# First quarter of w_in loaded ahead of two value loads, two pairs of odd-value copies moved from GpSimd to VectorE, a query copy moved up and one mask product repeated, in a fused windowed-attention and two-layer kernel

## The chip, the cores and the metric

The kernel runs on one core of one Trainium2 chip. The metric is the device time of one execution in microseconds (us); less is better. Times before the change: 294.75 us, the median of 5 runs (293.83 to 295.93).

The engines are named as in the profile: PE is TensorE, DVE is VectorE, ACT is ScalarE, POOL is GpSimd, SP is SyncE. All times of instructions below count from the start of the span of the profiled execution.

## What is computed

```python
# q, k, v: (8, 8, 576, 64) = batch, heads, sequence, head size; window 32
scores = (q @ k.T) / sqrt(64)
scores = where(abs(i - j) <= 32, scores, -1e9)
attn   = softmax(scores)
x      = (attn @ v) as (4608, 512)         # tokens x (heads * head size)
h      = x @ w_in                          # w_in (512, 2048)
g      = h * sigmoid(1.702 * h)
out    = g @ w_out                         # w_out (2048, 512), out (4608, 512) float32
```

## The kernel before

All work is one program for one core, in an order written out by hand: each engine runs its instructions in the order of the source, and waits on semaphores for what other engines or transfers produce. The 4608 tokens are 36 units of 128 tokens; two units make one tile of the two dense layers. The function `head` works off units 0 to 6 and the dense layers of the first tiles; `window(w)` then repeats for w = 4 to 19.

**Loads.** Nearly all are issued by POOL, in source order, and are cast to 16 bits on the way in. `load_heads("A")` and `load_heads("B")` bring the keys and queries of tokens 0 to 319 and 320 to 575 (a part of A comes through SP and ACT instead); `load_heads(1)` brings tokens 512 to 1023. `load_v(m)` brings the values of unit m into a tile `ve`; `load_v(4, 0)` brings only the first piece of unit 4, 64 rows, because unit 4 crosses from one batch into the next. `load_w_in(c)` brings the quarter c of w_in (512 of its 2048 columns, all of it for products d = 2c and 2c+1 of `layer1`), `load_w_out(c)` a quarter of w_out.

**Odd values.** A unit needs its values a second time, shifted by 64 tokens, in a tile `vo`. `odd_v(m, eng)` (L163) makes it with two copies of 64 x 528: the lower half of `ve` of unit m, and the upper half of `ve` of unit m+1. So `odd_v(2)` needs values 3, and `odd_v(3)` needs the first piece of values 4. Units 0 and 1 are copied by DVE and ACT, units 2 and 3 by POOL (before the change), the later ones by DVE.

**Block B, the stretch that the change touches.** After the values of units 0 and 1 the head prepares the keys and queries of block B for units 2 and 3. For each of four pairs of heads hp: `pair_heads` copies the loaded rows into an order fit for the transpose (tiles `kc`, `qc`, on DVE, 64 x 512); `rows_T` transposes them on PE into a PSUM bank (four transposes, L179) and copies the bank out to `kT` on DVE or to `qT` on ACT (L105). The banks are few: `"htho"[hp]` and `"hoth"[hp]` name them, "h" with two buffers, "t" and "o" with one. So the key transposes of hp = 2 wait for the copy `kT` of hp = 0, and the query transposes of hp = 2 (bank "t") wait for the copy `kT` of hp = 1 on DVE.

**Masks.** For units 0 to 3 the mask is not applied by a multiplication: `blind(u)` writes large negative numbers into both score banks (`sc`, eo = 0 and 1) by a product of an identity and the tile `neg`, 128 x 512, that starts the accumulation (L227), and `scores(u)` adds the products of keys and queries on top. Later units use a mask tile, made on POOL by `setup_mask` and `cut_mask`, and first read by `band(4)`.

**After block B.** `scores(2)`, `scores(3)`, then `layer1(0, 0)` (PE product with w_in, ACT for the activation, L313 and L315), `values(2)` (L273), `norm(2)` on DVE (L284, L285), `layer1(0, 1)`, `values(3)`, `norm(3)`, `x_T(2)` (transposes, L300), `layer1(0, 2)`, `x_T(3)`, `layer1(0, 3)` and from there a long run of products. `keep_busy(n)` issues n products of zeros of 128 x 512 whose results nobody reads (L418).

Of the kernel before, what the change touches and what calls it, by code (L numbers as in the profile page):

```python
# [21 lines left out]
SQ = 64  # L22
# [5 lines left out]
class _Kernel:  # L28
# [181 lines left out]
    def setup_neg(self):  # L210
# [4 lines left out]
        for b in range(2):  # L215
            for half in range(2):
# [2 lines left out]
                pool.affine_select(out=ap, in_=ap, compare_op=ALU.is_ge, fill=-30000.0, base=0,  # L219
                                   pattern=[[-sign, SQ]], channel_multiplier=sign)  # L220

    def blind(self, u):

        sc = self.sc[u] = [self.bank("a", [128, 8, SQ], F32, f"sc{eo}") for eo in range(2)]
        neg = self.neg.rearrange("k (o b) s -> k o b s", o=1).to_broadcast([128, 4, 2, SQ])
        for eo in range(2):
            self.nc.tensor.matmul(sc[eo].rearrange("k (h b) s -> k h b s", b=2), self.ident, neg,  # L227
                                  start=True, stop=False, skip_group_check=True)
# [192 lines left out]
    def head(self):  # L421

        nc, dve, act, pool = self.nc, self.nc.vector, self.nc.scalar, self.nc.gpsimd
# [8 lines left out]
            self.load_v(m)  # L432
        for c in "kq":
            self.load_heads("B", c)
        self.load_v(3)
        self.load_v(4, 0)
        for c in range(4):
            self.load_w_in(c)
        self.odd_v(2, pool)
        self.odd_v(3, pool)  # L440
        for c in (0, 2):
            self.load_w_out(c)
        self.setup_mask()
        self.cut_mask()
        for c in "kq":
            self.load_heads(1, c)
        self.load_w_out(1)
        self.load_v(4, 1)
        for m in range(5, 7):
# [30 lines left out]
        self.keep_busy(1, "h")  # L480
        for hp in range(4):
            self.pair_heads("k", "B", hp, dve)
        for hp in range(2):
            self.pair_heads("q", "B", hp, dve)
        for hp in range(4):
            self.rows_T("k", "B", hp, "htho"[hp], dve)
            if hp < 2:
                self.pair_heads("q", "B", hp + 2, dve)
            self.rows_T("q", "B", hp, "hoth"[hp], act)
        self.scores(2)  # L490
        self.scores(3)
        self.layer1(0, 0)
        self.values(2)
        self.norm(2)
# [278 lines left out]
```

## Time and profile before

| what | before |
|---|---|
| median of 5 runs, and their spread | 294.75 us (293.83 to 295.93) |
| the profiled execution: its time, its span | 295.93 us, 294.2 us |
| busy: PE, PEld, DVE, ACT, POOL | 286.7, 235.3, 187.3, 185.3, 104.1 us |
| mean granted TensorE clock | 0.994 |
| POOL, the loads of v3 and the first piece of v4 issued | 8.57 to 10.17 us |
| POOL, the four loads of w_in issued | 10.11 to 13.15 us |
| POOL, the copies for `odd_v(2)` and `odd_v(3)` | one at 13.07 us, three from 15.91 to 17.89 us |
| POOL, loads of w_out 0 and 2 issued | from 17.85 us |
| POOL, mask tile made | 19.31 to 21.52 us |

The profiled execution is the slowest of the five runs. The profile counts an engine as busy while an instruction of it is under way; PEld is PE's loading of weights. A line of the chain of waits gives start and length in us, then the engine, tile and source line that held the chain. A line of a timeline gives start, length, engine, line, operation, output and inputs, sizes and count, and in brackets the idle time before it and what ended it. In a table of stretches each engine has its busy time and, in brackets, its instructions; PEclk is the granted clock as a share of the full one.

### The profile page before, as it was taken

To read this page: it belongs to the slowest core of one execution; us is meant where nothing else is said; L and a number is where in the kernel's file an instruction comes from. 1 tells how busy PE (TensorE), PEld (TensorE's weight loads), DVE (VectorE), ACT (ScalarE), POOL (GpSimd) and SP (SyncE) were. 2 spreads that over 40 slices of the span, in tenths; PEclk is the share of its full clock that TensorE was granted. 3 is DMA by queue.
4 is the path that set the end of the run, shared out by engine and by line. 5 is a ranking of instruction groups with operands and counts; after the bars stand their busy time and mean duration, and the time that the engine had idled before them with its cause. 6 is when DMAs were issued, how large, how long until landed. Compare 5 with 4: busy or idle time off the path is not lost.

```text
span 294.2 us, 9542 instructions
## 1 busy us (share of the span) xinstructions
PE 286.7 (97%) x4020; PEld 235.3 (80%) x4020; DVE 187.3 (64%) x552; ACT 185.3 (63%) x306; POOL 104.1 (35%) x146
## 2 busy tenths in 40 slices
PE   7989999999999999999999999998999999999995
PEld 2558855775888888888888888887888888888884
DVE  3654358777485858585858585856585858583353
ACT  4666637786775757576767676766575757575330
POOL 8875435988634353433333434332000000000000
PEclk9979999999999999999999999999999999999999
DMA  9999999999999999999999999999925330303012
GB/s 147 145 207 206 200 184 129 193 141 143 151 167 164 160 148 152 174 142 203 101 165 129 170 117 142 149 139 153 161 38 145 38 109 3 108 6 107 2 71 71
DMA packets 145291, 38.83 MB, mean 132 GB/s; under 512 B 129888, under 2 KB 140896, under 8 KB 145248
## 3 DMA queue, kind: packets, MB, share of 16 engines
q0 software_dynamic: 97696, 18.16, 89.1%
q1 hardware_dynamic: 47104, 19.67, 41.3%
q8 instruction: 31, 0.51, 0.8%
q10 hardware_dynamic: 448, 0.39, 0.5%
q14 instruction: 12, 0.10, 0.2%
HBM read 36.96 MB, written 9.44 MB: 158 GB/s over the span
## 4 chain that ended last, share of the span: by engine, by line
PE 94%; DVE 2%; DMA 2%; ACT 1%; issue 1%; ACTq 0%; DVEq 0%
PE h_ps L313 43%; PE o_ps L375 32%; PE o_ps L325 7%; PE pv L273 4%; PE sc L245 4%; DMA q_raw<-in_q_dram 2%; PE tp L179 1%; PE tp L300 1%; DVE x L285 1%; ACT qT L105 1%; PE sc L227 0%; PE junk L418 0%; DVE o_sb L393 0%; DVE kT L105 0%; DVE qc L105 0%
## 5 line engine op out<-in xcount | busy, mean ns | idle before, releaser
L313 PE MATMUL h_ps<-xT,w_in_sb 128*128 128x256 bf16 x1152 | 136.3, 274 | 0.0
L315 ACT ACTIVATE g<-h_ps 128x512 f16<-128x512 f32 x144 | 85.7, 595 | 75.8 <-PE h_ps L313 74.4
L313 PEld LDWEIGHTS <-w_in_sb 128*128 128x128 bf16 x1152 | 112.6, 98 | 13.9
L160 POOL DMA_DIRECT2D ve<-in_v_dram x40 | 34.1, 858 | 83.8 <-PE pv L273 61.1
L375 PEld LDWEIGHTS <-gs 128*128 128x128 f16 x480 | 45.8, 98 | 5.8
L375 PE MATMUL o_ps<-w_sum,gs 128*128 128x256 f16 x360 | 44.3, 273 | 0.0
L251 ACT ACTIVATE p<-sc 128x512 bf16<-128x512 f32 x72 | 37.2, 604 | 2.7 <-PE sc L245 2.5
L375 PEld LDWEIGHTS <-g 128*128 128x128 f16 x360 | 34.1, 98 | 4.6 <-ACT g L315 0.2
L352 DVE TENSOR_TENSOR gs<-g 128x512 f16<-128x512 f16 x30 | 12.7, 425 | 39.1 <-ACT g L315 39.1
L285 DVE TENSOR_TENSOR x<-pv,rec 128x256 bf16<-128x256 f32 x72 | 30.6, 424 | 2.5
L375 PE MATMUL o_ps<-w_out_sb,g 128*128 128x256 f16 x240 | 29.0, 273 | 0.0
L105 DVE COPY part<-o_ps 128x256 f32<-128x256 f32 x45 | 19.1, 424 | 13.9 <-PE o_ps L375 12.6
L393 DVE TENSOR_TENSOR o_sb<-o_ps,part 128x256 f32<-128x256 f32 x45 | 19.0, 422 | 12.1 <-PE o_ps L375 11.4
L262 DVE TENSOR_TENSOR p<-p,mask 128x512 bf16<-128x512 bf16 x64 | 24.9, 427 | 1.2 <-ACT p L251 1.0
L147 POOL DMA_DIRECT2D qs<-in_q_dram x27 | 22.9, 868 | 3.2 <-DMA ks<-in_k_dram 2.8
L147 POOL DMA_DIRECT2D ks<-in_k_dram x27 | 22.8, 862 | 1.5 <-DMA ve<-in_v_dram 1.5
L325 PE MATMUL o_ps<-w_out_sb,g 128*128 128x512 f16 x96 | 23.2, 380 | 0.0
L105 DVE COPY vo<-ve 64x528 bf16<-64x528 bf16 x65 | 19.4, 298 | 2.0 <-DMA ve<-in_v_dram 0.5
L284 DVE RECIPROCAL rec<-pv 128x4 f32<-128x4 f32 x72 | 12.6, 175 | 12.0 <-PE pv L273 12.0
L412 ACT ACT_TABLE_LOAD x15 | 19.2, 1283 | 0.3
L251 ACT ACT_TABLE_LOAD x15 | 19.2, 1283 | 0.3
L273 PEld LDWEIGHTS <-p 128*64 128x64 bf16 x576 | 11.5, 111 | 7.3 <-DVE p L262 3.6
(70 smaller groups left out, 246.3 us busy)
## 6 DMA issues: line engine op xcount, KB each, us to landing
out_dram<-o_sb SPq DMA_DIRECT2D x34, 256.0 KB, 5.1
ve<-in_v_dram POOLq DMA_DIRECT2D x32, 128.0 KB, 5.8
ks<-in_k_dram POOLq DMA_DIRECT2D x22, 128.0 KB, 7.6
qs<-in_q_dram POOLq DMA_DIRECT2D x22, 128.0 KB, 9.1
w_in_sb<-in_moe_w_in_dram POOLq DMA_DIRECT2D x4, 512.0 KB, 10.8
w_out_sb<-in_moe_w_out_dram POOLq DMA_DIRECT2D x4, 512.0 KB, 12.1
ve<-in_v_dram POOLq DMA_DIRECT2D x8, 64.0 KB, 6.0
ks<-in_k_dram POOLq DMA_DIRECT2D x7, 64.0 KB, 6.7
```

What stands on the lines that cost most here:

```text
L105: (eng.copy if eng is self.nc.scalar else eng.tensor_copy)(out, in_)
L147: self.nc.gpsimd.dma_start(self.stage[key][off:off + m, n], src[b, :, s:s + m, :].rearrange("h s d -> s h d"))
L160: self.nc.gpsimd.dma_start(self.ve[m % NV][off:off + n, :, :self.D], self.v[b, :, s:s + n, :].rearrange("h s d -> s h d"))
L251: nc.scalar.activation(p[:, eo], sc[eo], AF.Exp, scale=self.scale)
L262: self.nc.vector.tensor_mul(pv, pv, msk.to_broadcast([128, 4, 2, SQ]))
L273: nc.tensor.matmul(acc[half][blk * 64:blk * 64 + 64, hh, :], p[:, h % 2, h // 2 * 2 + blk, :], vt[:, h, :D + 1], start=(hh == 0), stop=(hh ...
L285: nc.vector.tensor_mul(x[:, hs, :], acc[half][:, :, :D], rec[:, hs, :].to_broadcast([128, 4, D]))
L313: nc.tensor.matmul(hps[:, i, :], self.w_in_sb[:, kr, ff * 128:(ff + 1) * 128], self.xT[t][:, kr, :], start=(i == 0 and kr == 0), stop=(i = ...
L315: nc.scalar.activation(self.g[t][:, ffs[0]:ffs[1] + 1:ffs[1] - ffs[0], :], hps, AF.Gelu_apprx_sigmoid)
L325: nc.tensor.matmul(o_ps, self.g[t][:, ff, s * 128:(s + 1) * 128], self.w_out_sb[:, ff, :], start=(ff == 0), stop=(ff == self.NFF - 1))
L375: nc.tensor.matmul(self.part[t, key], x, y, start=(first and k == 0), stop=(k == 7), skip_group_check=True)
L412: self.nc.scalar.activation(self.spark, self.spark, AF.Gelu_apprx_sigmoid)
```

## The change

The loads: quarter 0 of w_in is issued before values 3 and the first piece of values 4 instead of after them. The two loads of keys and queries of block 1 (four transfers) are issued before the mask tile is made instead of after it. `odd_v(2)` and `odd_v(3)` are taken out of POOL's order (ahead of the loads of w_out) and given to DVE, after the scores of unit 3 and ahead of `norm(2)`. In block B the copy `qc` of hp = 2 is moved ahead of the first key copy; the copy of hp = 3 stays after it. Between the transposes of hp = 1 and hp = 2 PE repeats one product of the mask into the bank `sc` of unit 3, eo = 0, which already holds the same numbers.

```diff
+    def blind_again(self, u, eo):
+
+        neg = self.neg.rearrange("k (o b) s -> k o b s", o=1).to_broadcast([128, 4, 2, SQ])
+        self.nc.tensor.matmul(self.sc[u][eo].rearrange("k (h b) s -> k h b s", b=2), self.ident, neg,
+                              start=True, stop=False, skip_group_check=True)
...
             self.load_heads("B", c)
+        self.load_w_in(0)
         self.load_v(3)
         self.load_v(4, 0)
-        for c in range(4):
+        for c in range(1, 4):
             self.load_w_in(c)
-        self.odd_v(2, pool)
-        self.odd_v(3, pool)
         for c in (0, 2):
             self.load_w_out(c)
+        for c in "kq":
+            self.load_heads(1, c)
         self.setup_mask()
         self.cut_mask()
-        for c in "kq":
-            self.load_heads(1, c)
...
             self.pair_heads("k", "B", hp, dve)
-        for hp in range(2):
+        for hp in range(3):
             self.pair_heads("q", "B", hp, dve)
         for hp in range(4):
+            if hp == 2:
+                self.blind_again(3, 0)
             self.rows_T("k", "B", hp, "htho"[hp], dve)
-            if hp < 2:
-                self.pair_heads("q", "B", hp + 2, dve)
+            if hp == 0:
+                self.pair_heads("q", "B", 3, dve)
             self.rows_T("q", "B", hp, "hoth"[hp], act)
         self.scores(2)
         self.scores(3)
+        self.odd_v(2, dve)
+        self.odd_v(3, dve)
         self.layer1(0, 0)
```

## The prediction

> **What bounds the kernel now.** I read the page first, then the chain of waits between 14 and 25 us, then a table of stretches around it, then the timelines of DVE and POOL, and last the landing times of single transfers. The page:
>
> ```profile
> span 294.2 us, 9542 instructions
> PE 94%; DVE 2%; DMA 2%; ACT 1%; issue 1%; ACTq 0%; DVEq 0%
> ```
>
> PE holds 94% of the chain, and after 24.33 us it runs without a gap that counts. So a microsecond won in the head reaches the end, unless a transfer then comes late. The chain through block B:
>
> ```profile
> 15.36 0.23 PE tp L179 x4
> 15.59 0.02 issue
> 15.62 0.42 DVE kT L105
> 16.04 0.64 DVE qc L105
> 16.68 0.34 DVE kT L105
> 17.02 0.04 issue
> 17.06 0.29 PE tp L179 x4
> ...
> 18.17 0.58 PE sc L245 x40
> 18.75 1.82 PE h_ps L313 x8
> 20.56 0.58 PE pv L273 x8
> 21.14 1.36 PE h_ps L313 x8
> 22.50 0.38 PE pv L273 x16
> 22.88 0.33 PE tp L300 x4
> 23.21 0.87 PE h_ps L313 x8
> ```
>
> Two things are to be seen. A DVE copy of queries (0.64) stands between two key copies on the chain. And `layer1(0, 0)` takes 1.82 us for the eight products that take 0.87 at 23.21. The table of stretches says why; it is cut every 3.41 us, the length for which the half clock holds:
>
> ```profile
> 11.65:15.07 3.42, 3.26 (x32) 1.57 (x30) 2.02 (x9) 1.59 (x3) 2.14 (x4) 1.00 1.69 163
> 15.07:18.48 3.41, 2.43 (x95) 1.84 (x95) 2.79 (x8) 1.41 (x5) 2.45 (x4) 1.00 1.24 206
> 18.48:21.89 3.41, 3.41 (x54) 2.26 (x40) 0.85 (x4) 3.38 (x6) 3.06 (x12) 0.50 1.23 207
> ```
>
> After the length and the comma, the first number is PE's busy time, the third from the end the granted clock. The half clock fills 18.48 to 21.89, straight after the one stretch in which PE was busy for only 2.43 of 3.41 us. The two stretches before the first row shown, from 4.83 and from 8.24, have 3.06 and 3.08 us busy, and the clock stayed full behind them. So in this execution the limit lies between 2.43 and 3.06. How the stretches lie in other executions the trace does not show.
>
> **Part 1, the copy moved up and the POOL copies removed.** The timeline of all engines:
>
> ```profile
> 15.91 1.98 POOL L105 COPY vo<-ve 64x528 bf16<-64x528 bf16 x3 [2.13 <-DMA ve<-in_v_dram]
> 15.96 0.72 DVE L105 COPY qc<-qs 64x512 bf16<-64x512 bf16 x1
> ```
>
> This `qc` takes 0.72 us, beside a POOL copy; the two `qc` copies at 14.97 take 0.49 together, some 0.22 each from start to start. In the changed kernel the third `qc` follows them, at 15.41 to 15.69, while DVE would have waited for the first transposes anyway (ready at 15.59): up to 0.07 late. The first `kT` copy ends near 16.05 as before, one free `qc` follows (0.22 in place of 0.64), and the second `kT` copy ends near 16.64 in place of 17.02. The query transposes of hp = 2 start then: 0.38 us earlier. Everything to the end of the scores hangs on them, so scores end at 18.37, not 18.75. Between bounds: if only the order helped and not the missing POOL copy, 0.64 stays and nothing is won (0); if `kT` were not delayed at all, 0.42. I take 0.38.
>
> The Trainium skill ("SBUF — State Buffer", section "SBUF: two separate sides") says that DVE and GpSimd hold a shared pair of ports for a whole instruction, and also that a DVE copy which uses both ports keeps GpSimd from writing descriptors for its DMAs. The second half speaks against the change, which puts four such copies on DVE. The row nearest to it: POOL issued two value loads in 1.60 us at 8.57, while DVE made the copies of `odd_v(0)`, against 2.90 us for three at 4.33: no slowdown to see. By the rule POOL's issues could be about 1.2 us late there.
>
> **Part 2, the repeated product.** It is one more 128 x 512 on PE. In the chain three such products take 0.65 us, 0.22 each. PE stood idle before the key transposes of hp = 2 (0.17) and the query ones (0.69), so it lies in the gap: at most 0.1 on those key transposes, and nothing on the chain, since the query transposes wait for DVE until 16.68. If that cover were gone it would cost 0.22.
>
> **Part 3, the clock.** In the stretch 15.07 to 18.48 PE was idle for 0.98 us. The repeated product fills about 0.2, and 0.38 of the wait goes, its place taken by work that came later. The busy time comes to about 3.0, and the last 0.1 us is dense `layer1`. That is just at the lower edge of the stretches that kept the clock and far from 2.43, so I expect it to stay full. Then the chain from 18.75 to 24.33, 5.58 us, becomes three products at 0.87, two groups of values at 0.38 and two groups of transposes at 0.24: 3.85. That wins 1.73.
>
> The Trainium skill ("TensorE: Matmul & The Clock Gate", section "Why this matters for your kernels") asks only that PE has no idle gap over about 3 us. By that rule gaps of 0.17 and 0.69 us don't matter, and parts 2 and 3 would bring nothing: the sum would be 0.38. The granted clock in the table shows that they did matter. The same page (Part 4) says that transposes don't count as busy in the same way, which would fit this stretch.
>
> Does anything else hold that chain? I walked it at full clock. Scores end 18.37. `layer1(0, 0)` ends at 19.24. The exponentials (four in 2.06 us, first at 18.46 before, so 18.08) give unit 2 by 19.11 and unit 3 by 20.14. `values(2)` runs 19.24 to 19.62, `layer1(0, 1)` to 20.49, `values(3)` to 20.87, `x_T(2)` and `layer1(0, 2)` to 21.98. `norm(3)` ended 1.48 us after the start of `values(3)` before, so 21.97: in time. ACT loads its table (1.28) and runs the first activation by 22.06; `layer1(0, 3)` wants that bank at 22.22, not at 24.33. The gain at that point is 2.11 = 0.38 + 1.73.
>
> **Part 4, the loads.** The issue order decides the landing. In two narrow windows:
>
> ```profile
> w_in_sb<-in_moe_w_in_dram POOLq DMA_DIRECT2D x1, 512.0 KB, 8.0
> ve<-in_v_dram POOLq DMA_DIRECT2D x1, 64.0 KB, 6.7
> ```
>
> Quarter 0 was issued at 10.11 and landed at 18.1; the piece of v4 was issued at 9.37 and landed at 16.1; v3 (8.57, 7.2 us) at 15.8. Transfers landed in order of issue throughout the head. Exchanged, the three together still end at about 18.1: quarter 0 at about 17.5, v3 and v4 between 17.8 and 18.1. Quarter 0 is wanted at 18.37; it would have been in time even unmoved, so this brings 0 to 0.1. Quarter 1 (10.93 + 9.8 = 20.7) is wanted at 21.11.
>
> **Part 5, the copies on DVE.** Four copies at about 0.30 (six at 44.05 take 1.89). DVE was idle for 2.95 us before `norm(2)`. It finishes `kT` at 17.64; the first copy ends 17.95, the second waits for v3 and ends by 18.4 (`values(2)` wants it at 19.24), the last by 19.0. `norm(2)`, queued behind them, wants DVE at 19.53. So they cost nothing, with half a microsecond to spare. If v4 lands after 19.2, each microsecond costs one.
>
> **Part 6, POOL.** Without its 2.13 us wait POOL issues w_out earlier, but the transfers ahead of it fill the queue (205 GB/s), so landings stay. Mask building goes behind four load issues; its first reader is at 46.20. Two later transfers come near: queries of block 1 landed at 36.8 and PE wants their copy at 39.19 - 2.11 = 37.08; v7 landed at 44.8 and its copy stands ahead of `band(4)` on DVE, which would then end near 46.3, while PE reaches `values(4)` at 46.4. So about 2.2 us is all that can pass; beyond it these two hold PE.
>
> **The sum.** 295.93 - 2.11 = 293.82 us for the profiled execution, the slowest of five and 1.18 above the median. If all of that excess is the half clock, the changed kernel takes 293.82 in every run; if none, the median becomes 294.75 - 2.11 = 292.64. I take the middle, 293.2.
>
> **Rivals.** *The clock still drops.* If the limit is nearer to 3.06 than I think, or the window lies otherwise, only 0.38 is won: 294.4. For it: the margin of part 3 is thin. *The loads hold it back.* The two transfers of part 6 land half a microsecond to one later: about 294.2. *Slower:* transfers share the engines instead of landing in order, and the piece of v4 lands with quarter 1 at 20.7. Then the last copy ends at 21.0, `norm(2)` starts 1.5 us late, `x_T(2)` and the products wait, and PE's gap brings the half clock back (1.73): 293.2 + 3.2 = 296.4. It begins to count when v4 lands after 19.2, and decides from about 20.6. Against it: the strict order of landings. That the change does nothing of what it says needs `qc` to be slow without POOL too; then nothing of part 1 comes, and the clock decides alone.
>
> **How the numbers follow.** Full clock 0.66, at 292.6 to 293.8; clock still drops 0.15; later transfers take it 0.06; slower 0.13. A measurement of this kernel can tell about 0.5% (1.47 us) from no change, that is below 293.28 or above 296.22. Some 0.6 of the likeliest case lies below 293.28, and a little of the second: faster 0.42. The rest of these and the third are within: 0.45. Slower 0.13. The range 292.5 to 295.0 takes in the first three cases and leaves out the slower one and the tails.
>
> **What would show it.** Granted clock 1.00 in every stretch from 5 to 30 us; the `qc` copies at about 0.28 and no POOL copy of `vo`; `layer1(0, 0)` eight products in 0.87; `layer1(0, 3)` near 22.2; DVE's copies of `vo` waiting for v3 until about 18. I am wrong if a half clock stands anywhere in the head, if `norm(2)` starts behind a wait for `ve`, or if `kc`/`qc` of block 1 or `vo` of unit 6 hold PE near 37 or 46 us.

## The result and the profile after

| | before | after |
|---|---|---|
| median | 294.23 us (95 runs, 292.84 to 296.54) | 293.43 us (53 runs, 292.68 to 295.33) |
| ratio after to before, 95% interval | | 0.9969 [0.9959, 0.9979] |
| profiled execution: time, span | 295.93, 294.2 us | 293.43, 291.7 us |
| mean granted clock of the profiled execution | 0.994 | 0.999 |

The change wins 0.31% (0.21 to 0.41%): real, but within the 0.5% that the prediction counted as no change. The predicted 293.2 us is 0.2 us off, the range holds the time. That it is so near is partly luck. The prediction took 1.55 us off a median of 294.75 from five runs; with 95 runs the median before is 294.23, 0.52 lower, and the change took 0.80 off it. The two errors, 0.52 and 0.75, nearly cancel.

The chain of waits of the changed kernel, for the same stretch as before:

```profile
15.68 0.23 PE tp L179 x4
15.91 0.02 issue
15.93 0.42 DVE kT L105
16.36 0.19 DVE qc L105
16.55 0.34 DVE kT L105
16.89 0.04 issue
16.93 0.51 PE tp L179 x12
...
18.48 0.98 PE h_ps L319 x8
19.46 0.38 PE pv L279 x16
19.83 0.98 PE h_ps L319 x8
20.81 0.38 PE pv L279 x16
21.19 0.33 PE tp L306 x4
21.52 0.87 PE h_ps L319 x8
22.39 0.24 PE tp L306 x4
22.63 11.35 PE h_ps L319 x104
```

(Line numbers behind L221 are six higher than before, behind the head nine.) The `qc` copy between the two `kT` copies holds the chain for 0.19 us instead of 0.64. The eight products of `layer1(0, 0)` take 0.98 instead of 1.82. The long run of products starts at 22.63, before at 24.33: 1.70 us earlier, although block B itself happened to start 0.32 later (15.68 against 15.36). The table of stretches, cut at the same times as before:

```profile
15.07:18.48 3.41, 3.23 (x100) 2.16 (x100) 2.98 (x9) 1.53 (x5) 1.10 (x3) 1.00 1.66 184
18.48:21.89 3.41, 3.41 (x57) 2.72 (x58) 2.68 (x11) 3.38 (x6) 1.85 (x3) 1.00 1.24 207
```

PE is busy for 3.23 us (before 2.43), and the clock behind it is full. VectorE's timeline, with the copies taken over from POOL:

```profile
17.82 1.56 DVE L105 COPY vo<-ve 64x528 bf16<-64x528 bf16 x4
19.75 0.18 DVE L290 RECIPROCAL rec<-pv 128x4 f32<-128x4 f32 x1 [0.37 <-PE pv L279]
```

The four copies are done at 19.38, and `norm(2)`, whose first instruction is the second line, waits for PE, not for them: 0.37 us to spare, 0.5 had been worked out.

The two profiled executions lie 2.50 us apart, the medians only 0.80. Of the 2.50, 1.70 come from the head, and 1.11 from a line of the chain of before that the change has nothing to do with:

```profile
202.87 1.11 issue
```

PE stood still there in the middle of `values`, and the profile names nothing that it waited for. After has 0.31 us of such and other small pieces more than before elsewhere (1.70 + 1.11 - 2.50).

One of the runs of before that were made beside the experiments, of 298.16 us, was in a slow state and is left out of all counts and means below.

### The profile page after: what moved, and what is told of

Same layout as the page of the kernel before. It is cut to its first block, busy times and chain, and to the rows that moved or that the text cites. A ratio compares the mean times of both kernels' runs of the same rounds, so it can differ in the third digit from the quotient of the medians.

```text
span 291.7 us, 9542 instructions
## 1 busy us (share of the span) xinstructions
PE 285.6 (98%) x4021; PEld 234.5 (80%) x4021; DVE 190.1 (65%) x556; ACT 185.1 (63%) x306; POOL 101.9 (35%) x142
## 4 chain that ended last, share of the span: by engine, by line
PE 93%; DVE 2%; DMA 2%; POOL 1%; issue 1%; ACT 0%; POOLq 0%; DVEq 0%
PE h_ps L319 43%; PE o_ps L381 32%; PE o_ps L331 7%; PE sc L251 4%; PE pv L279 4%; DMA ve<-in_v_dram 2%; PE tp L179 1%; PE tp L306 1%; DVE x L291 1%; PE sc L233 0%; DVE o_sb L399 0%; POOL ve L160 0%; POOL neg L219 0%; DVE kT L105 0%; POOL qs L137 0%
## 5 line engine op out<-in xcount | busy, mean ns | idle before, releaser
L105 DVE COPY vo<-ve 64x528 bf16<-64x528 bf16 x69 | 22.7, 328 | 3.1 <-DMA ve<-in_v_dram 1.6
L418 ACT ACT_TABLE_LOAD x15 | 19.2, 1283 | 0.3
L257 ACT ACT_TABLE_LOAD x15 | 19.2, 1283 | 0.3
```

Source lines behind the costliest of these rows:

```text
L105: (eng.copy if eng is self.nc.scalar else eng.tensor_copy)(out, in_)
L257: nc.scalar.activation(p[:, eo], sc[eo], AF.Exp, scale=self.scale)
L418: self.nc.scalar.activation(self.spark, self.spark, AF.Gelu_apprx_sigmoid)
```

## The experiments

Theory: in every execution block B is some 0.4 us shorter; in some executions of before, but not in all, a half clock follows block B and costs more than a microsecond, and the change makes these rare. Rivals: the half clock is the whole matter, and the repeated product cures it; the clock has no part; the order of the copies is what helps, not the engine; the new order of loads does it.

Each execution lists its mean granted clock. One half-clock stretch of 3.41 us in a span of 294 takes it to 0.994, so executions at 0.995 or less are counted below as having one; where in the span it lies, only the profiled ones show. "Full" is the mean of the others with its standard error; "at full clock" means these executions. "Block B" is read from the profiled execution: from the first key transposes of block B to the start of the long run of products. The runs of before that were made beside the experiments are pooled. It is left blank where the chain of waits does not run through those transposes.

| kernel | executions | with a half clock | median us | full, mean us | block B, us |
|---|---|---|---|---|---|
| before | 97 | 19 | 293.99 | 293.82 +- 0.06 | 8.97 (half clock) |
| changed, first 54 | 54 | 2 | 293.43 | 293.39 +- 0.07 | 6.95 |
| changed again (e10) | 12 | 0 | 293.19 | 293.43 +- 0.19 | 6.96 |
| e1, product alone | 12 | 3 | 293.95 | 293.78 +- 0.15 | 7.41 |
| e2, changed without product | 12 | 1 | 293.52 | 293.46 +- 0.15 | |
| e3, odd values on DVE alone | 12 | 4 | 293.59 | 293.26 +- 0.16 | 7.11 |
| e4, changed, w_in back | 12 | 0 | 293.28 | 293.42 +- 0.11 | 6.96 |
| e5, order alone | 12 | 2 | 293.41 | 293.32 +- 0.08 | |
| e6, before, gaps filled | 12 | 0 | 294.13 | 294.11 +- 0.15 | 7.30 |
| e7, before, less filling | 12 | 4 | 294.05 | 293.76 +- 0.17 | |

### e1, the product alone

```diff
+            if hp == 2:
+                self.blind_again(3, 0)
             self.rows_T("k", "B", hp, "htho"[hp], dve)
```

> The kernel before with the repeated product alone. Theory (the gain is a shorter block B plus a half clock that falls away in those executions that had it): the product lies in PE's gap, costs nothing, and lifts the busy time of the stretch ahead of the half clock from 2.43 to about 2.65 us. Executions with a half clock in the head become fewer but not none; median 0 to 0.5 us below before. Rival A (the product is what counts, the clock limit lies just above 2.43): half clocks vanish, and the whole gain of 0.8 us is there. Rival B (the clock has no part): time as before within 0.2 us.

Ratio to before 1.0016 [0.9986, 1.0047]. At full clock as before (293.78 against 293.82), and 3 of 12 executions have a half clock, before 19 of 97. Rival A falls: the product alone does not cure it. That half clocks become fewer, as the theory had it, is not seen either. In its place the product costs nothing that can be measured (the error is 0.16 us), as predicted.

### e2, the changed kernel without the product

```diff
-            if hp == 2:
-                self.blind_again(3, 0)
             self.rows_T("k", "B", hp, "htho"[hp], dve)
```

> The changed kernel without the repeated product. Theory: block B is as short as in the changed kernel (scores end some 0.4 us earlier than before), busy time of the stretch about 3.0 instead of 3.2 us; half clocks come back in some executions, median 0 to 0.4 us above the changed kernel. Rival A: all half clocks of the kernel before come back, median 0.5 us or more above the changed kernel. Rival B: no difference, within 0.15 us.

Ratio to before 0.9982 [0.9964, 1.0000]. At full clock 293.46, the changed kernel 293.39; one half clock in 12. In PE's timeline the first key transposes of block B and the long run of products are 6.87 us apart, in the changed kernel 6.86. So the product is not needed for the shorter block B, and whether it makes half clocks rarer (2 of 66 with it, 1 of 12 without) these counts can't tell. Its profile shows what comes next when PE is early; the timeline of PE:

```profile
38.16 0.34 PE L179 MATMUL tp<-ident,qc 128*128 128x128 bf16 x3 [0.24 <-DVE qc L105]
```

PE waits 0.24 us for the queries of block 1, whose transfer landed at 37.7. The prediction had named this transfer as one of the two that bound the gain.

### e3 and e5, each half of the change to block B alone

e3 moves the odd values and leaves the order, e5 the reverse:

```diff
-        self.odd_v(2, pool)
-        self.odd_v(3, pool)
...
         self.scores(3)
+        self.odd_v(2, dve)
+        self.odd_v(3, dve)
```

> The kernel before with odd values of units 2 and 3 copied by VectorE instead of GpSimd, nothing else. Theory: the query copy that took 0.72 us takes about 0.28, the copies kT of hp 1 to 3 come 0.4 us earlier although the order of copies is the old one, and the half clock becomes rarer; median 0.3 to 0.8 us below before. Rival C (the order of the copies is what helps): less than 0.1 us. Rival D (the four copies hold back norm(2)): slower by 0.3 us or more, with norm(2) behind a wait for ve.

```diff
-        for hp in range(2):
+        for hp in range(3):
             self.pair_heads("q", "B", hp, dve)
...
-            if hp < 2:
-                self.pair_heads("q", "B", hp + 2, dve)
+            if hp == 0:
+                self.pair_heads("q", "B", 3, dve)
```

> The kernel before with the query copy of hp 2 moved up, nothing else: GpSimd still copies the odd values of units 2 and 3. Theory (the POOL copies are what lengthens block B): the copy that now meets the first POOL copy takes some 0.6 to 0.7 us in its new place, the second kT copy ends where it did, and executions at full clock take the time of before within 0.15 us. Rival C (the order helps by itself): executions at full clock 0.3 to 0.4 us below before.

Ratios to before: e3 0.9999 [0.9973, 1.0024], e5 0.9991 [0.9968, 1.0015], with 4 and 2 half clocks in 12 executions. At full clock they are at 293.26 and 293.32, as low as the whole change. So I was wrong on e5: each half alone brings about 0.4 us, and errors of 0.16 and 0.08 can't tell whether both together bring more. The profiles have block B at 7.41 us in e1, 7.11 in e3 and 6.95 with both. On e3 the theory was right about the copy, but half clocks did not become rarer (4 in 12). VectorE's timelines say what happened to the copy. First e3, then e5:

```profile
16.10 0.34 DVE L105 COPY qc<-qs 64x512 bf16<-64x512 bf16 x1
```

```profile
15.34 0.69 DVE L105 COPY qc<-qs 64x512 bf16<-64x512 bf16 x3 [0.85 <-DMA qs<-in_q_dram]
15.95 0.41 DVE L105 COPY kT<-tp 128x256 bf16<-128x256 bf16 x1
16.29 0.38 DVE L105 COPY qc<-qs 64x512 bf16<-64x512 bf16 x1
```

In e3 the query copy in its old place takes 0.34 us (before 0.72), because no POOL copy of values is beside it. What cost 0.64 on the chain can be read by setting the POOL copy beside the query copy, in before (its `qc` at 15.96 stands in the prediction), in e1 and in e5:

```profile
15.91 0.62 POOL L105 COPY vo<-ve 64x528 bf16<-64x528 bf16 x1 [2.13 <-DMA ve<-in_v_dram]
```

```profile
16.09 0.62 POOL L105 COPY vo<-ve 64x528 bf16<-64x528 bf16 x1
16.22 0.64 DVE L105 COPY qc<-qs 64x512 bf16<-64x512 bf16 x1
```

```profile
15.90 0.62 POOL L105 COPY vo<-ve 64x528 bf16<-64x528 bf16 x1 [2.16 <-DVE qc L105]
```

The query copy ends at 16.68, 16.86 and 16.67, each time 0.15 us after the POOL copy. In the profiles of before, e1, e5, e6 and e7 nine query copies began while a POOL copy ran, and all nine ended 0.14 or 0.15 us after it. So the query copy waits for the end of the POOL copy, and how long it takes depends on when it starts: 0.72 us when it begins 0.05 after the POOL copy, 0.38 when it begins 0.39 after it (e5), 0.29 near its end (e6, at 16.05). Only e3 takes the POOL copies away. In e5 three query copies are through by 16.03 and the fourth still meets a POOL copy, though late in it. Against e7, which has the order of before and whose queries landed as late (15.31 us), e5 is 0.25 us shorter from the query copies at 15.34 to the long run (7.53 and 7.78 us), 0.15 of it by this later meeting. Why the order alone brings as much as it does over all its executions is not shown.

### e4, quarter 0 of w_in back in its old place

```diff
-        self.load_w_in(0)
         self.load_v(3)
         self.load_v(4, 0)
-        for c in range(1, 4):
+        for c in range(4):
             self.load_w_in(c)
```

> The changed kernel with quarter 0 of w_in back behind values 3 and 4. Theory: quarter 0 lands near 18.1 us, just before layer1(0, 0) wants it; values 3 and 4 land 2 us earlier, so VectorE's copies wait for nothing; time as the changed kernel within 0.15 us. Rival E: layer1(0, 0) waits for quarter 0, in executions with a late landing above all; median 0.2 to 0.5 us above the changed kernel.

Ratio to before 0.9979 [0.9963, 0.9996], at full clock 293.42. The first part of the change named in its title brings nothing that can be measured, as the prediction had it (0 to 0.1). The other change to the loads, keys and queries of block 1 ahead of the mask tile, was not taken out by itself; e3 and e5 reach the time of the changed kernel at full clock without it.

### e6 and e7, more and less filling, on the kernel before

e6 puts one repeated product ahead of the key transposes of hp 2 and two behind them; e7 takes out the four products of zeros ahead of `x_T(1)`:

```diff
+            if hp == 2:
+                self.blind_again(3, 0)
             self.rows_T("k", "B", hp, "htho"[hp], dve)
+            if hp == 2:
+                self.blind_again(3, 0)
+                self.blind_again(3, 1)
```

> The kernel before with three repeated products in PE's two idle gaps of block B, one ahead of the key transposes of hp 2 and two ahead of the query transposes of hp 2; nothing else changed. Theory: the stretch is busy for about 3.1 us, no execution has a half clock in the head (before: 6 of 35), chain as before: median as the executions of before at full clock, 293.8 to 293.9 us. Rival A (the limit lies elsewhere): half clocks as often as before. Rival F: the added products lie in the way, 0.2 us slower at full clock.

```diff
-        self.keep_busy(4, "a")
         self.x_T(1, "a", act)
```

> The kernel before without the four products of zeros ahead of x_T(1), which fill PE while norm(1) runs. Theory: PE is busy for about 0.9 us less in the stretch from 11.7 to 15.1 us, so half clocks in the head become frequent (half of the executions or more, before 6 of 35), and one costs 1.3 to 1.7 us; executions at full clock as before within 0.15 us. Rival B (the clock has no part): time as before.

Ratios to before: e6 0.9995 [0.9973, 1.0017], e7 1.0005 [0.9985, 1.0026]. e6 has no half clock in 12, but is slower at full clock: in its profile the products hold PE until 17.10, when the copy that the query transposes wait for was done at 16.66. Rival F fits, in the profile and in size (0.29 +- 0.16 us). That no half clock came fits the theory, but at the share of before 12 executions would have none in 7% of the cases, so it is not shown. e7 has 4 half clocks in 12, fewer than expected; against 19 of 97 that says little. That the clock has a price is plain: of the 97 executions of before, the 19 with a half clock have a mean of 295.05 us, the other 78 of 293.82, so one costs 1.23 us. It is not one fixed price: in e1 the three with a half clock are 3.0 us above the others, in e9 the nine 0.75.

### e8, the next loads reordered

```diff
-        for c in (0, 2):
-            self.load_w_out(c)
+        self.load_w_out(0)
         for c in "kq":
             self.load_heads(1, c)
+        self.load_w_out(2)
...
-        for m in range(5, 7):
+        for m in range(5, 8):
             self.load_v(m)
         self.load_w_out(3)
-        self.load_v(7)
...
-        for n in range(4):
-            self.w_sums(n, 0)
         for c in "kq":
             for hp in range(4):
                 self.pair_heads(c, 1, hp, dve)
+        for n in range(4):
+            self.w_sums(n, 0)
```

> The changed kernel with keys and queries of block 1 loaded ahead of quarter 2 of w_out, values 7 ahead of quarter 3 of w_out, and VectorE's w_sums after the copies of block 1 instead of before. Theory (the queries of block 1 and values 7 land just in time in the changed kernel): the queries land near 34 us instead of 37, VectorE's wait for values 7 goes; PE wins 0 to 0.25 us in executions that are early. Rival G: quarter 2 of w_out, now behind, holds PE near 38 us: 0.3 us or more slower.

Ratio to before 1.0005 [0.9987, 1.0023]; at full clock 293.89 +- 0.10 (11 executions): the gain of the change is gone. The loads did what was expected, the queries of block 1 were there at 34.15 us instead of 36.69. Rival G is not what its profile shows. Block B takes 6.96 us, and PE runs as in e10, the same changed kernel, within 0.1 us until the scores near 195 us (195.37 against 195.30; in the first profile of the changed kernel 195.90); then it has one idle piece of 0.77 us for which nothing is named, like the 1.11 us of before. Whether that is why the kernel is slower in most executions is open.

### e9, block B laid out anew

```diff
-        self.keep_busy(4, "a")
-        self.x_T(1, "a", act)
         self.blind(2)
+        self.keep_busy(2, "h")
+        self.x_T(1, "h", act)
         self.blind(3)
-        self.keep_busy(1, "h")
...
-        for hp in range(3):
-            self.pair_heads("q", "B", hp, dve)
+        for hp in range(2):
+            self.rows_T("k", "B", hp, "ht"[hp], dve)
+        self.blind_again(3, 0)
         for hp in range(4):
-            if hp == 2:
-                self.blind_again(3, 0)
+            self.pair_heads("q", "B", hp, dve)
+        for hp in range(2):
+            self.rows_T("q", "B", hp, "ho"[hp], act)
+        for hp in (2, 3):
             self.rows_T("k", "B", hp, "htho"[hp], dve)
-            if hp == 0:
-                self.pair_heads("q", "B", 3, dve)
             self.rows_T("q", "B", hp, "hoth"[hp], act)
```

> The changed kernel with block B laid out anew: two of the mask products replace the four products of zeros, the transposes and copies kT of hp 0 and 1 come ahead of the query copies, so that only two kT copies stand behind the landing of the queries. Theory (after the change the loads are the next limit): scores end up to 0.8 us earlier, but layer1(0, 2) then waits for quarter 1 of w_in (about 20.7 us) and the transposes of block 1 for their queries (about 37 us); of the 0.8 us at most 0.3 arrives, time 0 to 0.3 us below the changed kernel. Rival H (PE is still the limit there): 0.6 us or more below. Rival I (less filling): half clocks come back, in a quarter of the executions or more.

Ratio to before 1.0004 [0.9987, 1.0021], median 294.33 us, and 9 of 12 executions have a half clock. Rival I holds. In the profiled execution the clock stayed full, and the loads held PE, as the theory has it. From its chain of waits:

```profile
10.96 11.97 DMA w_in_sb<-in_moe_w_in_dram
...
22.98 1.05 PE h_ps L319 x8
```

Quarter 1 of w_in, issued at 10.96, landed at 22.93 and not near 20.7, and PE waited 1.56 us for it. Nor did the scores end earlier by much: `layer1(0, 0)` began at 18.31, in e10 at 18.29. A version faster than the changed kernel did not come of this.

### e10, the changed kernel again, and e11, values 4 late

> The changed kernel again, on the chip of this call, for a comparison with the other two. Theory: about 293.4 us, 0.4 to 0.5 us below before at full clock, at most one execution of twelve with a half clock in the head. Rival: a part of the difference to before was a difference of chips, and less than 0.2 us is left.

Ratio to before 0.9980 [0.9961, 0.9998]; 293.43 us at full clock, no half clock: as the first 54. The runs of before beside it are at 293.87 at full clock, 0.44 +- 0.22 above, so a difference between chips is not what made the gain, as far as this error goes.

e11 tests the slower rival of the prediction by its own mechanism:

```diff
+        self.load_w_in(1)
         self.load_v(4, 0)
-        for c in range(1, 4):
+        for c in range(2, 4):
             self.load_w_in(c)
```

> The changed kernel with the first piece of values 4 loaded behind quarter 1 of w_in as well. Theory: it lands near 20.7 us instead of 18; VectorE's last copy vo ends near 21.0, norm(2) starts some 1.3 us later, x_T(2) and the products behind it wait for it: 1.0 to 1.5 us slower than the changed kernel, and 1.3 more in the executions in which PE's gap brings a half clock. Rival J (the wait is hidden elsewhere): within 0.2 us.

Ratio to before 1.0007 [0.9990, 1.0024]; mean 294.33 us, 0.9 above the changed kernel. The chain of waits:

```profile
10.90 9.95 DMA ve<-in_v_dram
...
20.87 0.29 DVE vo L105
```

The piece of v4 landed at 20.85, and `norm(2)` started at 21.09 instead of 19.75: 1.34 us late. PE's long run of products began at 23.70 instead of 22.63. The price is a little under the 1.0 to 1.5 us expected, and the half clock did not come back in any of 12 executions. So the rival's mechanism is real, at 0.9 and not 3.2 us; in the change itself the piece landed in time.

## Why the prediction was right, and what was off in it

**Part 1, 0.38 us.** Right in size: executions at full clock fell from 293.82 +- 0.06 to 293.39 +- 0.07, 0.43 +- 0.09 us, and block B from 7.41 (e1, the order of before at full clock) to 6.95 us. The cause, a query copy that waits for the end of a POOL copy, is shown by the nine meetings and by e3. The bound "if only the order helped and not the missing POOL copy, 0.64 stays and nothing is won" was wrong: e5 wins about 0.4 us with the POOL copies in place. The Trainium skill ("SBUF — State Buffer", section "SBUF: two separate sides") has the two engines take turns on a shared pair of ports, each holding it for a whole instruction; these rows agree, with the query copy ending 0.15 us behind the POOL copy, and 0.27 us long in the changed kernel, where none is beside it.

**Part 2.** Right: the product costs nothing that can be measured (e1).

**Part 3, 1.73 us.** For the profiled execution the sum was nearly right: from its start to the long run block B became 2.02 us shorter (8.97 to 6.95), where 2.11 had been worked out. Three things in it were off.

First, the size. From the end of the scores to the long run of products, the changed kernel takes 4.15 us (18.48 to 22.63), not the 3.85 of the sum: two groups of eight products take 0.98 and not 0.87, two transposes 0.33 and not 0.24. Against the 5.58 of before, a half clock costs 1.43, and the executions say 1.23.

Second, and larger, how often. The step that failed is the one from the profiled execution to the median: "I take the middle" let the half clock account for half of its excess over the median. It has a half clock, but 78 of 97 executions of before have none. The change takes the share from 19 of 97 to 2 of 66. Worked out: 0.20 x 1.23 less 0.03 x 1.87 is 0.18 us of the mean; with 0.43 from the executions at full clock 0.61, against 1.55 predicted. Counted directly, the means of all these executions are 294.06 and 293.46. The ratio on record, 0.9969, means 0.9 us of 294.2, with 0.6 at the near end of its interval; its 95 runs of before have a mean of 294.36, and their clocks are not on record, so where the other 0.3 comes from is open.

Third, the reason given for the half clock. That the limit lies between 2.43 and 3.06 us of busy time was read from one execution, and the other profiles don't bear it out: stretches with 1.85 us (e9), 2.42 (e11) and 2.45 (e7) kept the clock (the last section has the rows of e7 and e9). So the step from PE's idle 0.98 us to the half clock was argued and not shown. What is shown is that half clocks are rarer with the shorter block B; why, and by which edit, is open: 6 of 24 with only one half of the block B change, 3 of 90 with both (e2, e4, e10 and the first 54), with or without the product.

**Parts 4 to 6.** The moved quarter brings nothing (e4). The piece of v4 landed near 18.7 us (issued at 10.2, 8.5 us later), at least 0.6 behind what was worked out (17.8 to 18.1) and still ahead of the 19.2 from which it counts. The four copies on DVE fit, with 0.37 us to spare, and cost when their input is late (e11). The two transfers of part 6 are where they were predicted: 0.24 us of waiting in e2; and v7 in the changed kernel, from VectorE's timeline:

```profile
45.07 0.29 DVE L105 COPY vo<-ve 64x528 bf16<-64x528 bf16 x1 [1.15 <-DMA ve<-in_v_dram]
```

**The rivals.** "The clock still drops" was right for few executions of the changed kernel, and wrong as a picture: it took for granted that before drops always. It also took for granted a limit on busy time that the other profiles don't show. The slower rival was excluded by the landing of v4, with half a microsecond to spare.

## What to carry to other kernels

One profiled execution shows one draw of the clock. Before a half-clock stretch is put into a sum, look at the mean granted clock of the other executions: it says in how many the stretch exists, and the mean moves by that share of its price only. When an instruction takes more than twice the time of its neighbours of the same shape, look for what runs beside it on the other engine, and compare where the two end. A limit read from one stretch of one profile is a guess until other profiles bear it out.

## What the runs showed of the hardware

The busy time in the profile does not decide the clock by itself. In before, 2.43 us of 3.41 were followed by a half clock. In the profiled executions of e7 and e9, cut by the times at which their clocks change, stretches with 2.45 and 1.85 us were not (third number from the end: 1.00 in the next stretch too). First e7, then e9:

```profile
12.93:16.34 3.41, 2.45 (x26) 1.24 (x27) 2.76 (x12) 0.92 (x3) 1.15 (x3) 1.00 1.65 187
16.34:19.76 3.42, 2.65 (x88) 2.08 (x87) 1.81 (x5) 2.22 (x7) 3.30 (x6) 1.00 1.24 206
```

```profile
19.73:23.14 3.41, 1.85 (x30) 1.34 (x31) 2.49 (x9) 2.84 (x4) 0.40 (x1) 1.00 1.24 207
23.14:26.56 3.42, 3.42 (x35) 3.10 (x34) 0.96 (x4) 1.72 (x3) 2.96 (x11) 1.00 1.24 207
```

The stretch of e9 even has the idle piece of 1.56 us in it, where PE waited for w_in; in before the longest was 0.69. The stretch of before holds mainly transposes and scores of 64 columns, e7's products of 512 and e9's products of 256. That this is the difference is an idea, not tried.

A query copy on VectorE (64 x 512) that began beside a copy of odd values on GpSimd (64 x 528, 0.62 us) ended 0.14 or 0.15 us after it, in all nine meetings in five profiles.

PE also has idle pieces near 158 or 202 us that nothing in the profile explains: 1.11 us in before, 0.38 in e1, 0.58 in e3, 0.72 in e6, 0.77 in e8, none of this size in the other eight profiles. They are as large as the effect measured here, and differ from one profile to the next.
